# Local scores and AV as full 128x128 matmuls in batches 1 to 3, with loads and casts of batches 2 and 3 at other places

## The chip, the cores and the metric

The kernel runs on one core of a Trainium2 chip. The metric is the device time of one execution in microseconds, of which three runs of the kernel before are given below. A core has five engines with an instruction stream each: TensorE (PE, matmuls, with weight loads shown apart as PEld), VectorE (DVE), ScalarE (ACT), GpSimd (POOL) and SyncE (SP, which issues most of the DMAs here). PE writes to PSUM, eight banks of 512 fp32 columns on 128 partitions; ACT and DVE read it from there.

## What is computed

Block-sparse attention, and a gated feed-forward layer behind it. Shapes: 4 batches, 8 heads, 768 positions, head size 64; d_model 512, d_ff 2048.

```python
k_sum = k.reshape(B, H, nb, 32, D).max(axis=3)          # 24 block maxima of the keys
v_sum = v.reshape(B, H, nb, 32, D).mean(axis=3)         # 24 block means of the values
scores_l = where(|pos_q - pos_k| < 16, scale * q @ k.T, -1e9)
scores_s = scale * q @ k_sum.T + log(32)
a = softmax(concat([scores_l, scores_s]))
attn = a @ concat([v, v_sum])
x = attn, heads side by side                            # 3072 x 512
h = x @ w_in
out = (h * sigmoid(beta * h)) @ w_out
```

## The kernel before

**Attention of one batch.** The 768 positions are cut into 12 query tiles of 64 (`QT`). A tile needs a window of 96 keys (`NK`) and the 24 block maxima, 120 columns, padded to 128: `kw[g][:, m, :]` holds them for tile m of head pair g (`G` = 4 pairs; the two heads of a pair lie on partitions 0 to 63 and 64 to 127). `scores` (L429) makes, for one pair and one half u of the positions (a *score unit*), twelve matmuls of 64 rows by 64 columns into a two-bank PSUM tile `big[..]`, head h in bank h; `weigh` (L443) takes the Exp on ACT into a tile `e`, and `mask_e` (L449) multiplies by the band mask on DVE. `av_mm` (L503) multiplies blocks of e of 64 queries with the values: `ve` holds them in windows for even tiles, `vo` for odd ones (shifted by 64, made by DMAs from `ve`), with a column of ones for the softmax sum and, on partitions 96 to 119, the block means. The means come from `vm_all` (L481, 28 matmuls of 32 columns), are copied to `vm_sb` by DVE and ACT in turn, and spread into `vo` and `ve` by `spread` (L491, DVE). `av_pair` (L863) does both halves of a pair, and `norm` (L529) divides on DVE. `x_dma` (L549) turns the result into `xT` by a transposing DMA (one pair in batch 3 by PE, `x_both`). Batch 0 has forms of its own (`scores0`, `av_split`).

**Feed-forward of one batch.** `h_tile` (L602) makes 16 tiles of h (PE, then Silu on ACT). The product with w_out is a plain one for most of batch 0 (`o_atom`, L623, four matmuls of 512 columns) and else seven half-size products (`product`, L661, eight matmuls of 256 columns each; numbers 1 to 7), for which `h_sums` (L647) and `w_sums` (L655) make sums of quarters on DVE, and `gather` (L682) adds the results up on ACT, DVE and POOL. Products go to PSUM tiles `one0`, `one1`, `acc0`, `acc1`; `SLOTS` says which: 4 goes to acc0, 3 and 5 to acc1. acc0 also serves `vm_all` in batches 2 and 3.

**Order.** A list `main` of steps (8 of `h_two`, 16 of `h_half`, 16 of `o_atom`, 7 products, and for each later batch 16 of `h_step` and 21 products) is run in turn. Everything else is a side step with a place in the table `AT` (L12): a side step at 28.05 is emitted behind main step 28. Each engine runs its instructions in the order emitted and waits for what they need, so a place in the table sets the order on every queue, not a time. So the o_atoms are steps 24 to 39, the h stage of batch 1 is steps 47 to 62, its products 63 to 83, and so on, 37 steps a batch. Names in `AT`, with the batch as the last letter: kl, ql, vl loads (SP); kc, qc, vc casts (POOL); kd, qd transposing DMAs (SP); win, kx, ks build `kw` and the maxima (DVE, DVE, POOL); vo the shifted values; sc, mk, vm, sp, av, xd the steps above; hs, ws the sums.

Of the kernel before, what the change touches and what calls it, by code (L numbers as in the profile page):

```python
# [17 lines left out]
    'clear': [6.428, 6.644],  # L18
    'kt': [10.122, 8.68],
    'km': [17.109, 13.223, 16.831, 23.85],  # L20
    'qt': [26.508, 26.967],
    'late': [32.254],
    'ws': [23.447, 26.164, 38.352, 39.431],
    'hs0': [36.284, 36.98, 42.604, 40.783],
    'vc1': [26.849, 25.757, 27.058, 30.017],
    'vo1': [27.153, 26.475, 30.624, 30.427],
    'exp1': [26.482],
    'sc1': [28.05, 28.06, 30.05, 30.06, 31.438, 31.448, 33.219, 33.904],
    'mk1': [28.082, 28.092, 30.899, 30.909, 32.558, 32.75, 33.826, 34.448],
    'silu1': [34.957],  # L30
    'vm1': [30.622],
    'sp1': [31.039, 33.384],
    'av1': [35.473, 35.88, 37.299, 37.483],
    'xd1': [36.323, 36.794, 40.874, 39.001],
    'hs1': [52.172, 56.695, 58.36, 62.056, 63.409],
    'kl2': [31.49, 27.509, 31.14, 31.359],
    'ql2': [44.528, 45.846, 48.477, 49.061],
    'vl2': [48.656, 50.666, 53.32, 55.633],
    'kc2': [46.766, 47.002, 48.913, 52.382],
    'kd2': [47.896, 48.564, 50.287, 53.981],  # L40
    'win2': [48.822, 54.925, 59.06, 64.294],
    'kx2': [50.116, 57.618, 60.611, 66.447],
    'ks2': [57.494, 58.64, 61.796, 70.807],
    'qc2': [47.142, 55.572, 56.241, 59.845],
    'qd2': [53.645, 55.686, 56.34, 64.339],
    'vc2': [60.103, 63.811, 64.371, 63.63],
    'vo2': [60.676, 64.705, 67.24, 64.464],
    'exp2': [62.362],
    'sc2': [64.902, 64.912, 67.132, 67.349, 69.423, 69.507, 71.144, 71.507],
    'mk2': [64.907, 67.547, 69.019, 69.041, 70.656, 70.74, 74.611, 74.621],  # L50
    'silu2': [83.261],
    'vm2': [69.738],
    'sp2': [70.773, 71.834],
    'av2': [73.1, 73.251, 76.15, 76.759],
    'xd2': [73.535, 75.753, 77.844, 80.713],
    'hs2': [88.697, 93.491, 96.096, 98.876, 99.837],
    'kl3': [70, 68.576, 66.104, 68.383],
    'ql3': [85.72, 83.832, 83.154, 85.128],
    'vl3': [87.046, 86.957, 91.359, 92.448],
    'kc3': [83.124, 84.172, 85.522, 85.86],  # L60
    'kd3': [83.91, 86.33, 85.635, 89.794],
    'win3': [91.341, 93.68, 91.196, 100.991],
    'kx3': [93.659, 96.229, 96.044, 103.349],
    'ks3': [93.765, 97.224, 99.448, 104.103],
    'qc3': [90.383, 91.035, 87.741, 88.767],
# [15 lines left out]
    'mask2': [46.27],  # L81
# [21 lines left out]
def kernel(  # L103
# [39 lines left out]
    NEG = -30000.0  # L143
    assert d_model == H * D and out.shape == (B * S, d_model) and NK + nb <= P
# [104 lines left out]
    mask = const.tile([P, NT, QT], bf16, name="mask")  # L249
# [44 lines left out]
    def more_masks():  # L294
        nc.vector.tensor_copy(out=mask[:], in_=band[:, None, :].to_broadcast([P, NT, QT]))
        nc.vector.memset(mask[0:W, 0], 0.0)
        nc.gpsimd.affine_select(out=mask[:, NT - 1], in_=mask[:, NT - 1], compare_op=ALU.is_ge, fill=0.0,
                                base=QT + W - 1, pattern=[[0, QT]], channel_multiplier=-1)
        nc.vector.memset(mask[NK:NK + nb], 1.0)

    mask2 = const.tile([P, NT, QT], bf16, name="mask2")

    def turn_mask():
        nc.vector.tensor_copy(out=mask2.rearrange("p m (c f) -> p m c f", c=2), in_=mask.rearrange("p m (f c) -> p m c f", c=2))

# [6 lines left out]
    qn = [const.tile([P, S], bf16, name=f"qn{g}") for g in range(G)]  # L312
# [116 lines left out]
    def scores(b, g, u, bg):  # L429
        s = big[bg]  # L430
        for j in range(HT):
            m = u * HT + j
            for h in range(2):
                o = s[:, h, j * QT:(j + 1) * QT]
                if b > 1:
                    nc.tensor.matmul(o.rearrange("p (c f) -> p c f", c=2), kw[g][h * D:(h + 1) * D, m, :], q_tile2(g, h, m),
                                     start=True, stop=True)
                else:
                    nc.tensor.matmul(o, kw[g][h * D:(h + 1) * D, m, :], q_tile(g, h, m), start=True, stop=True)
# [529 lines left out]
```

## Time and profile before

| | |
|---|---|
| three runs | 215.21, 216.53, 216.9 us; median 216.53 us |
| span of the profiled execution | 213.4 us, clock 1.00 |
| its time outside the span | not given; median less span is 3.1 us |
| busy, share of the span | PE 95%, PEld 66%, DVE 65%, ACT 56%, POOL 29% |
| instructions | 5774 |

The page of the profile has the busy time of each engine, the span in 40 slices, the DMA queues, the chain of work that ended last, and the costliest groups. A timeline row has start, length, engine, line, operation, tiles written and read, shapes and count; in brackets the idle time before it and what ended that. A matmul's length in the trace is a latency, some 0.2 us; what a stream of them costs is read from start to start. The chain before goes through PE for 54% of the span, DVE 14%, DMA 14%.

### The profile page before, as it was taken

How to read it: one execution, taken by the hardware profiler on the slowest of the kernel's cores; microseconds unless marked ns; L12 is line 12 of the kernel's file. 1: busy time of each engine (PE TensorE's matmuls, PEld its weight loads, DVE VectorE, ACT ScalarE, POOL GpSimd, SP SyncE). 2: the span in 40 equal slices, each digit the busy share in tenths (PEclk: the TensorE clock that was granted, in tenths of full speed). 3: DMA queues.
4: the chain of work that ended last, by engine and by line, in shares of the span. 5: the costliest groups of instructions: out<-in, count | busy, mean ns of one | idle time of the engine just before them, and what ended most of it. 6: DMA issues, size and time to landing. Idle time of an engine off the chain costs nothing.

```text
span 213.4 us, 5774 instructions
## 1 busy us (share of the span) xinstructions
PE 202.9 (95%) x2393; PEld 140.1 (66%) x2393; DVE 139.5 (65%) x323; ACT 119.0 (56%) x182; POOL 62.0 (29%) x94
## 2 busy tenths in 40 slices
PE   7778999999998999999999999999999999999993
PEld 2366856565554586556888875667788855668882
DVE  4297574799839992677889920999789704464232
ACT  2246986579489121966883137778772229772210
POOL 7609990002620009423520153461600100000111
PEclk9999999999999999999999999999999999999999
DMA  6998999999877995999979999999834820000242
GB/s 119 183 219 150 185 207 207 206 208 214 113 187 199 243 202 179 236 152 202 170 152 223 194 272 272 210 193 194 123 129 27 185 99 3 0 0 3 98 98 98
DMA packets 78393, 33.92 MB, mean 159 GB/s; under 512 B 60688, under 2 KB 75424, under 8 KB 78368
## 3 DMA queue, kind: packets, MB, share of 16 engines
q1 hardware_dynamic: 61968, 23.92, 55.2%
q0 software_dynamic: 7424, 7.34, 21.4%
q10 hardware_dynamic: 8976, 2.30, 7.3%
q8 instruction: 18, 0.29, 0.6%
q14 instruction: 7, 0.06, 0.1%
HBM read 27.37 MB, written 6.29 MB: 158 GB/s over the span
## 4 chain that ended last, share of the span: by engine, by line
PE 54%; DVE 14%; DMA 14%; SPq 5%; ACT 4%; issue 4%; POOL 3%; POOLq 0%; DVEq 0%
PE big L600 18%; PE one L664 11%; PE acc L664 8%; DMA vst<-in_v_dram 8%; PE big L578 4%; PE one L615 3%; DMA krow<-in_k_dram 3%; ACT e L447 3%; DVE kw L371 2%; DVE w_out_sb L337 2%; DMA qst<-in_q_dram 2%; DVE km L357 2%; DVE e L451 2%; POOL ve L456 1%; SPq L210 1%
## 5 line engine op out<-in xcount | busy, mean ns | idle before, releaser
L600 PE MATMUL big<-xT,w_in_sb 128*128 128x384 bf16 x360 | 60.5, 326 | 0.0
L600 PEld LDWEIGHTS <-w_in_sb 128*128 128x128 bf16 x384 | 37.5, 98 | 25.1 <-issue 0.7
L611 ACT ACTIVATE h_sb<-big,beta_sb 128x768 bf16<-128x768 f32 x45 | 39.6, 904 | 25.7 <-PE big L600 25.6
L664 PEld LDWEIGHTS <-h_sb 128*128 128x128 bf16 x320 | 30.6, 98 | 4.9 <-issue 0.5
L645 POOL TENSOR_TENSOR o_sb<-p,u 128x256 f32<-128x256 f32 x10 | 7.3, 727 | 88.9 <-DVE u L645 77.0
L447 ACT ACTIVATE e<-big,bias 128x768 bf16<-128x768 f32 x32 | 27.3, 900 | 6.2 <-PE big L426 4.3
L664 PE MATMUL one<-w_out_sb,h_sb 128*128 128x256 bf16 x240 | 30.4, 273 | 0.2 <-ACT p L368 0.2
L664 PEld LDWEIGHTS <-s_sb 128*128 128x128 bf16 x240 | 23.2, 98 | 2.8
L645 DVE TENSOR_TENSOR s_sb<-h_sb 128x768 bf16<-128x768 bf16 (+2 forms) x16 | 7.8, 487 | 23.5 <-ACT h_sb L611 23.5
L645 DVE TENSOR_TENSOR u<-one,p 128x256 f32<-128x256 f32 x20 | 8.4, 422 | 15.8 <-PE one L664 15.5
L456 POOL CAST ve<-vst 128x832 bf16<-128x832 f32 (+2 forms) x16 | 14.1, 901 | 14.9 <-DMA vst<-in_v_dram 12.5
L368 ACT COPY o_sb<-one 128x256 f32<-128x256 f32 (+1 forms) x14 | 6.1, 433 | 18.4 <-PE one L664 10.0
L451 DVE TENSOR_TENSOR e<-e,mask 128x768 bf16<-128x768 bf16 x24 | 13.7, 597 | 3.9 <-ACT e L447 3.6
L615 PE MATMUL one<-w_out_sb,h_sb 128*128 128x512 bf16 x64 | 15.2, 380 | 0.0
L365 POOL COPY kw<-km 128x288 bf16<-128x288 bf16 x12 | 7.5, 628 | 24.1 <-DVE km L357 14.4
L361 DVE TENSOR_REDUCE km<-kT 128x24 bf16<-128x768 bf16 x12 | 11.2, 944 | 1.8 <-ACT kT L368 1.8
L538 DVE TENSOR_TENSOR xn<-big,r 128x768 bf16<-128x768 f32 x12 | 11.5, 957 | 0.4
L578 PE MATMUL big<-xT,w_in_sb 128*128 128x384 bf16 x64 | 11.7, 327 | 0.0
L664 PE MATMUL acc<-t_sb,h_sb 128*128 128x256 bf16 x80 | 10.9, 273 | 0.0
L568 POOL CAST qn<-qst 128x768 bf16<-128x768 f32 x8 | 7.4, 938 | 10.2 <-DMA qst<-in_q_dram 6.9
L664 PE MATMUL one<-t_sb,s_sb 128*128 128x256 bf16 x80 | 10.4, 273 | 0.0
L664 PE MATMUL acc<-t_sb,s_sb 128*128 128x256 bf16 x80 | 10.4, 273 | 0.0
(145 smaller groups left out, 309.1 us busy)
## 6 DMA issues: line engine op xcount, KB each, us to landing
out_dram<-o_sb SPq DMA_DIRECT2D x19, 256.0 KB, 2.7
vst<-in_v_dram SPq DMA_DIRECT2D x13, 336.0 KB, 5.1
kst<-in_k_dram SPq DMA_DIRECT2D x8, 384.0 KB, 5.0
qst<-in_q_dram SPq DMA_DIRECT2D x8, 384.0 KB, 4.6
w_in_sb<-in_moe_w_in_dram POOLq DMA_DIRECT2D x4, 512.0 KB, 8.0
w_out_sb<-in_moe_w_out_dram POOLq DMA_DIRECT2D x4, 512.0 KB, 13.1
vo<-ve SPq DMA_DIRECT2D x12, 107.2 KB, 2.4
vst<-in_v_dram SPq DMA_DIRECT2D x3, 416.0 KB, 7.1
```

The costliest lines, as they stand in the source:

```text
L361: nc.vector.tensor_reduce(out=km[g][:, NK:NK + nb], in_=kT[g][:, W:W + S].rearrange("p (n f) -> p n f", f=block), op=ALU.max, axis=AX.X)
L365: eng.tensor_copy(out=kw[g][:, :, NK:NK + nb], in_=km[g][:, None, NK:NK + nb].to_broadcast([P, NT, nb]))
L447: nc.scalar.activation(out=e[:], in_=s[:, :, 0:HS], func=ACTF.Exp, bias=bias[:, 0:1], scale=scale)
L451: nc.vector.tensor_mul(out=e.rearrange("p h (m q) -> p h m q", q=QT), in0=e.rearrange("p h (m q) -> p h m q", q=QT), in1=(mask2 if b > 1 e ...
L456: eng.tensor_copy(out=ve[:, g, lo:hi, 0:D], in_=vst[g][:, lo:hi])
L538: nc.vector.tensor_mul(out=x[:, 3 * us[0]:3 * us[0] + 3 * n].rearrange("p (k j) h d -> p k (j h) d", k=n), in0=tv[:, :, :, 0:D], in1=r[:, ...
L578: nc.tensor.matmul(t[:, 0:HS], w_in_sb[:, ki, i * P:(i + 1) * P], xT[:, ki, 0:HS], start=(ki == 0), stop=(ki == k1 - 1))
L600: nc.tensor.matmul(o, w_in_sb[:, ki, i * P:(i + 1) * P], x, start=(ki == 0), stop=(ki == k1 - 1))
L611: nc.scalar.activation(out=o, in_=t, func=ACTF.Silu, scale=beta_sb[:, i:i + 1])
L615: nc.tensor.matmul(t[:, 0:hi - lo], h_sb[:, n, ms * P:(ms + 1) * P], w_out_sb[:, n, lo:hi], start=(n == 0), stop=(n == k2 - 1))
L645: eng.tensor_tensor(out=o, in0=a, in1=b, op=op)
L664: nc.tensor.matmul(SLOTS[n], a[:, j, t * P:(t + 1) * P], b[:, j], start=(j == 0 and n not in (2, 3, 7)), stop=(j == J2 - 1), skip_group_ch ...
```

## The change

Scores of batches 1 to 3 use a query tensor `qz` that holds, for each pair, head 0 on the upper partitions and zeros below, then zeros above and head 1 below. One matmul over all 128 rows then gives both heads: six matmuls of 128 columns a unit instead of twelve of 64. The tiles of a unit go to the two banks in turn by their parity. The Exp is written into blocks of `epad` that have zeros between them, so that a 128-column piece holds the queries of an even tile and zeros, or zeros and those of an odd tile; AV of a pair of tiles is then two full matmuls that add up in PSUM (start, stop) instead of two of 64 columns side by side. There are as many AV matmuls as before. `qz` and `epad` are cleared once (`clear_q`, `clear_e`, and a memset at the start). In batch 1 the q copies from PSUM are four of half the partitions on ACT and four on DVE; in batches 2 and 3 the transposing DMA writes as before, and `q_fix` moves the second head over on DVE and clears its place on POOL. The masks have 14 tiles instead of 12, and move to the pool that is closed at `late_tiles`; the turned mask is made early. Four tiles of e serve batches 1 to 3 (six batch 0) instead of eight, and three output tiles instead of four.

```diff
-    'clear': [6.428, 6.644],
+    'clear': [5.9, 6.644, 6.9, 6.1, 7.2, 7.3],
-    'qt': [26.508, 26.967],
+    'qt': [24.4, 24.5],
-    'ws': [23.447, 26.164, 38.352, 39.431],
+    'ws': [27.0, 27.5, 33.7, 39.431],
-    'sc1': [28.05, 28.06, 30.05, 30.06, 31.438, 31.448, 33.219, 33.904],
+    'sc1': [28.1, 28.6, 29.9, 30.6, 33.1, 33.6, 34.7, 35.3],
-    'av1': [35.473, 35.88, 37.299, 37.483],
+    'av1': [32.9, 34.6, 36.6, 37.9],
...
-    'ql2': [44.528, 45.846, 48.477, 49.061],
+    'ql2': [32.0, 33.0, 34.0, 38.5],
-    'win2': [48.822, 54.925, 59.06, 64.294],
+    'win2': [48.0, 48.9, 49.8, 50.7],
-    'vc2': [60.103, 63.811, 64.371, 63.63],
+    'vc2': [43.5, 44, 44.5, 45.5],
-    'sc2': [64.902, 64.912, 67.132, 67.349, 69.423, 69.507, 71.144, 71.507],
+    'sc2': [64.5, 64.9, 66.1, 66.8, 70.9, 72.2, 74.0, 75.0],
-    'vm2': [69.738],
+    'vm2': [68.2],
-    'av2': [73.1, 73.251, 76.15, 76.759],
+    'av2': [70.4, 73.0, 76.4, 78.0],
-    'vc3': [95.284, 91.652, 97.814, 103.191],
+    'vc3': [79, 80, 81, 82.5],
...
+    def clear_q(gs):
+        nc.vector.memset(qz[D:P, 0, gs], 0.0)
+    def clear_e():
+        for n in range(NE[1]):
+            nc.vector.memset(epad[:, n, :, 1], 0.0)
...
+    epad = eb.rearrange("p (n a b q) -> p n a b q", n=NE[1], b=3, q=QT)
...
+    def q_fix(g):
+        nc.vector.tensor_copy(out=qz[D:P, 1, g], in_=qz[D:P, 0, g])
+        nc.gpsimd.memset(qz[D:P, 0, g], 0.0)
...
-            for h in range(2):
-                o = s[:, h, j * QT:(j + 1) * QT]
...
-                    nc.tensor.matmul(o, kw[g][h * D:(h + 1) * D, m, :], q_tile(g, h, m), start=True, stop=True)
+            o, q = s[:, j % 2, j // 2 * P:(j // 2 + 1) * P], qz[:, :, g]
...
+            nc.tensor.matmul(o, kw[g][:, m, :], q, start=True, stop=True)
...
+    def av_mm(b, g, u, t):
+        tv = t[:, 0:AVW].rearrange("p (j h e) -> p j h e", j=3, h=2)
+        e = et[(b, g, u)][1].rearrange("p a b q -> p a (b q)")
+        for j in range(3):
+            for h in range(2):
+                for par in range(2):
+                    nc.tensor.matmul(tv[:, j, h], e[:, 2 * j + h, par * QT:par * QT + P],
+                                     (vo if par else ve)[:, g, h * J6 + 3 * u + j, 0:D + 1], start=(par == 0), stop=(par == 1))
+        release(b, g, u)
...
+    SB = (2, 1, 2, 1, 2, 1, 1, 2)
...
-    at("qt", [lambda i=i: qt_pe(1, (2 * i, 2 * i + 1), 1 + i, (dve_cp, act_cp)) for i in range(2)])
+    at("qt", [lambda i=i: qt_pe(1, (i, i + 2), 1 - i, (act_cp, dve_cp)[i]) for i in range(2)])
-        at("av" + n, [lambda g=g, b=b: av_pair(b, g, big[1 + g % 2]) for g in range(G)])
+        at("av" + n, [lambda g=g, b=b: av_pair(b, g, big[(1 + g % 2) * (b > 1)]) for g in range(G)])
```

`SB` is the two-bank tile of each score unit. By the last line the AV pairs of batch 1 all write big0, where `vm_all` of batch 1 also goes.

How the rows move, at three places. First DVE ahead of batch 1's scores, from the second copy of x in batch 0 to the scaling of w_out; qz is the query tensor, eb the storage of the Exps, mask_173 the turned mask. Before:

```order
L371 COPY xT<-one_79 128x2x384
L295 COPY mask<-band 128x768
L296 MEMSET mask 16x32
L299 MEMSET mask 24x768
L337 TENSOR_SCALAR w_out_sb<-w_out_sb,inv_beta 128x512 x4
```

Now:

```order
L312 MEMSET eb 128x6x32 x4
L384 COPY xT<-one_76 128x2x384
L296 COPY mask<-band 128x896
L297 MEMSET mask 16x64
L300 MEMSET mask 24x896
L305 COPY mask_173<-mask 128x896
L308 MEMSET qz 64x768 x2
L350 TENSOR_SCALAR w_out_sb<-w_out_sb,inv_beta 128x512 x4
```

The turned mask and two memsets have come in ahead of the scaling, and so of all key work behind it.

Second, DVE in batch 1 from the q copies on; e or eb are the Exps, vm_sb the block means, t_sb the sums of `w_sums`. Before:

```order
L371 COPY qn_177<-big_80 128x768
L371 COPY qn_179<-big_81 128x768
L451 TENSOR_TENSOR e<-e,mask 128x768 x2
L371 CAST vm_sb<-big_85 32x2x64 x2
L451 TENSOR_TENSOR e<-e,mask 128x768 x2
L496 COPY vo<-vm_sb 32x2x6x64 x2
L496 COPY ve<-vm_sb 32x2x6x64 x2
```

Now:

```order
L384 COPY qz<-big_82 64x768 x4
L686 TENSOR_TENSOR t_sb<-w_out_sb 128x2048
L686 TENSOR_TENSOR t_sb<-w_out_sb,t_sb 128x2048
L481 TENSOR_TENSOR eb<-eb,mask 128x2x6x64 x3
L384 CAST vm_sb<-big_82 32x2x64 x2
L481 TENSOR_TENSOR eb<-eb,mask 128x2x6x64
L525 COPY vo<-vm_sb 32x2x6x64 x2
L525 COPY ve<-vm_sb 32x2x6x64 x2
```

The q copies are four, and the two t_sb sums, which stood ahead of them, now stand between them and the masks. Further on in the same stretch, from the masks of pair 3 (s_sb is a sum of `h_sums`, xn the normed result, here of pair 2), now:

```order
L481 TENSOR_TENSOR eb<-eb,mask 128x2x6x64 x2
L686 TENSOR_TENSOR s_sb<-h_sb 128x8x128
L578 RECIPROCAL r<-big_82 128x12
L579 TENSOR_TENSOR xn<-big_82,r 128x768
L686 TENSOR_TENSOR s_sb<-s_sb,h_sb 128x8x128
```

Before, the first of these sums stood behind the norms of pairs 0 and 1, and each norm read a big tile of its own turn; now the norm of pair 2 stands behind the masks of pair 3 and a sum.

Third, DVE in batch 2 around `vm_all`, whose result is in acc_1797 or acc_1789, the tile of product 4; u is the sum that product 7 ends in. Before:

```order
L645 TENSOR_TENSOR u_1931<-one_79,p_1821 128x256
L645 TENSOR_TENSOR o_sb<-acc_1797,u_1931 128x256
L645 TENSOR_TENSOR o_sb<-acc_1798,u_1867 128x256
L451 TENSOR_TENSOR e<-e,mask_176 128x768 x2
L371 CAST vm_sb<-acc_1797 32x2x64 x2
```

Now:

```order
L686 TENSOR_TENSOR u_1898<-one_76,p_1814 128x256
L686 TENSOR_TENSOR o_sb<-acc_1789,u_1898 128x256
L384 CAST vm_sb<-acc_1789 32x2x64 x2
L525 COPY vo<-vm_sb 32x2x6x64 x2
L525 COPY ve<-vm_sb 32x2x6x64 x2
L686 TENSOR_TENSOR o_sb<-acc_1790,u_1841 128x256
```

By 'vm2' at 68.2, PE makes `vm_all` straight behind step 68, which is product 7 of the first third; before, product 3 and two score units stood in between. DVE's read of acc and its copy of the means now follow each other.

166 lines of the change are left out of this document (92 added, 74 removed).

## Prediction

> **What bounds the kernel now.** I read the clock and span first, then the stretches, PE's instructions in order of time, the chain, and last the waits and the groups by form. One core, clock 1.00, span 213.4 us. The three runs have a median of 216.53 us (215.21 to 216.9), so 3.1 us lie around the span; I make the sum on the span and add 3.1. About 1%, 2.2 us, is what a measurement of this kernel can tell from no change.
>
> ```profile
> 40.00:58.00 18.00, 17.49 (x209) 10.55 (x208) 17.84 (x33) 11.97 (x21) 4.24 (x6) 1.00 1.18 189
> 58.00:75.00 17.00, 15.77 (x275) 8.80 (x274) 12.50 (x29) 11.45 (x17) 1.87 (x3) 1.00 0.88 201
> ```
>
> A row gives the stretch, its length, and the busy us of PE, PEld, DVE, ACT and POOL. PE is all but full, so what is added to PE is added to the end. From 40 to 58 us DVE is full too (17.84 of 18.00): two engines bind there at once. Scores and AV of batches 1 to 3 stand in three stretches, whose edges PE's timeline gives:
>
> ```profile
> 52.20 0.59 PE L615 MATMUL one<-w_out_sb,h_sb 128*128 128x512 bf16 x2
> 80.39 0.81 PE L600 MATMUL big<-xT,w_in_sb 128*128 128x384 bf16 x4
> 101.36 0.82 PE L664 MATMUL acc<-t_sb,h_sb 128*128 128x256 bf16 x6
> 125.09 0.81 PE L600 MATMUL big<-xT,w_in_sb 128*128 128x384 bf16 x4
> 146.07 0.60 PE L664 MATMUL acc<-t_sb,h_sb 128*128 128x256 bf16 x4
> 170.46 0.81 PE L600 MATMUL big<-xT,w_in_sb 128*128 128x384 bf16 x4
> ```
>
> A (batch 1, beside the output product of batch 0) is 28.19 us, B (batch 2 beside the products of batch 1) 23.73, C 24.39. What a burst of small matmuls costs there:
>
> ```profile
> 103.00 0.27 PE L664 MATMUL one<-w_out_sb,h_sb 128*128 128x256 bf16 x1
> 103.20 0.52 PE L436 MATMUL big<-qn,kw 64*128 64x64 bf16 x24
> 103.66 1.05 PE L664 MATMUL one<-t_sb,s_sb 128*128 128x256 bf16 x8
> ...
> 68.60 0.88 PE big L511 x48
> ```
>
> Two score units (24 matmuls on half the rows) take 0.46 us from start to start, 19 ns each: two run side by side. Products follow each other every 0.109 us (8 in 0.87), but 0.20 pass before the burst: 0.10 to empty the array as the tile shape changes; leaving it is inside the 0.46. An AV burst of 48 takes 0.88 the same way. A batch has four score bursts and two AV bursts: 4 x 0.56 + 2 x 0.98 = **4.2 us** of PE.
>
> **The change: PE's work.** Scores become 48 matmuls of 128 columns on all rows, AV 96 with a 128x128 stationary block and 65 columns, neither of them tiled. Both shapes stand in the trace elsewhere:
>
> ```profile
> 35.97 0.50 PE L860 MATMUL one<-identity,xn 128*128 128x128 bf16 x6
> L860 PE MATMUL one<-identity,xn 128*128 128x128 bf16 x12 | 1.0, 219 | 0.0
> 23.54 0.35 PE L519 MATMUL one<-vm_one,e 128*128 128x65 bf16 x6
> L519 PE MATMUL one<-vm_one,e 128*128 128x65 bf16 x24 | 1.4, 194 | 0.0
> ```
>
> Six in 0.50 of which the last is 0.219: 56 ns a step. Six in 0.35, the last 0.194: 31 ns. So scores 48 x 56 = 2.7, AV 96 x 31 = 3.0, and the block means of v (vm_all, 32 columns wide, still tiled) now pay their own 0.1: **5.8 us, +1.6 a batch, +4.9 in all**. The emptying that goes (six times 0.1 in, and as much out) is already in this: full matmuls do twice the array work that two tiles shared. Bounds: the step can't fall under the column rate (0.109 / 256 = 0.43 ns: 54 and 28 ns; -0.4 a batch), and AV's pairs, which now add into one bank, could cost the 56 ns of the other shape (+2.4 a batch). I take 31, the same shape on the same e.
>
> [...]
>
> **Waits that go.** The two long ones, and what else stands in A:
>
> ```profile
> 54.88 1.55 PE L384 MATMUL big<-identity,qrow 96*64 96x96 bf16 x64
> ...
> 58.89 0.53 PE L439 MATMUL big<-qn,kw 64*128 64x64 bf16 x24 [0.62 <-ACT qn L368]
> 59.35 1.90 PE L615 MATMUL one<-w_out_sb,h_sb 128*128 128x512 bf16 x8
> 61.18 0.52 PE L439 MATMUL big<-qn,kw 64*128 64x64 bf16 x24
> 61.63 0.58 PE L485 MATMUL big<-ve,A_avg 128*32 128x128 bf16 x28
> ...
> 66.42 0.35 PE L439 MATMUL big<-qn,kw 64*128 64x64 bf16 x12 [0.44 <-ACT e L447]
> ```
>
> 59.35 to 61.18 is 1.83 for eight output matmuls and the change of shape: 0.217 each, 0.87 for four. In A 64 of them, 56 products at 0.109, the q transposes (1.6 with their change of shape), vm_all (0.5) and the 4.2 make 26.3 of 28.19: 1.9 are waits. In B 168 products (18.4), vm_all and the 4.2 leave 0.7, in C, with 0.3 for x_both, 1.0. I let all 3.6 us go: q is now copied by ACT before its Exp table, keys and values of batches 2 and 3 come some 20 steps earlier, and kw and km are built in the h stages, not between the masks. If nothing new waited, the span would grow by 4.9 - 3.6 = 1.3.
>
> **Waits that come, A.** DVE is the engine queued up there, and the change adds to it ahead of its scale and key work:
>
> ```profile
> L299 DVE MEMSET mask<- 24x768 bf16 x1 | 0.7, 698 | 0.4 <-POOL mask L297 0.4
> L304 DVE COPY mask<-mask 128x768 bf16<-128x768 bf16 x1 | 0.6, 550 | 0.0
> 56.20 1.81 DVE L371 COPY qn<-big 128x768 bf16<-128x768 bf16 x2
> ```
>
> clear_q is two memsets of 768 words (0.70 each, time going by words, not partitions), the turned mask 0.55 x 14/12 = 0.64, longer masks 0.1: +2.1. The q copies are now four of half the partitions and the same 768 columns: 0.87 a piece, +1.7. Two more stand in waits that DVE has anyway:
>
> ```profile
> DVE xT L371 <- PE one L860: 1.6, 2, 0.9
> DVE beta_sb L325 <- PE one L324: 1.4, 1, 1.4
> ```
>
> clear_e (four of 192 words, 0.7) fits the wait for x_two (half of 1.6), the memset of qz at the start (1536 words, 1.4) that for beta; uncovered they cost at most their length once. DVE was through with q and the first two T sums at 58.0; the order is changed, the sum not, so now 61.85. Then come:
>
> ```profile
> 63.58 0.29 DVE L371 CAST vm_sb<-big 32x128 bf16<-32x128 f32 x1 [1.03 <-ACT vm_sb L368]
> 63.90 1.03 DVE L451 TENSOR_TENSOR e<-e,mask 128x768 bf16<-128x768 bf16 x2
> 64.94 0.63 DVE L496 COPY vo<-vm_sb 32x768 bf16<-32x768 bf16 x2
> 65.49 0.62 DVE L496 COPY ve<-vm_sb 32x768 bf16<-32x768 bf16 x2
> ```
>
> three masks (1.5), the vm_sb pair with ACT's copy between (0.9), a mask (0.5), spread(0) (1.2): 66.0. PE reaches AV of pair 0 at 52.2 + 9 x 0.87 + 1.6 + 4 x 0.34 + 0.6 + 0.2 = 63.8. **It waits 2.2.** Behind it on PE stand the scores of pairs 2 and 3, so ACT runs dry too. Next late is AV of pair 3: all four AV pairs now use the one tile big0, and the norm of pair 2 stands on DVE behind both masks of pair 3 and an h sum. From 66.0 PE needs 8.0 to get there (74.0). ACT meanwhile:
>
> ```profile
> 64.67 3.28 ACT L447 ACTIVATE e<-big,bias 128x768 bf16<-128x768 f32 x4
> 70.70 3.00 ACTq L553 DMA_TRANSPOSE xT<-xn  x2
> ```
>
> two Exps of pair 2 until 69.9, x_dma of pair 0 on ACT's own queue 1.3 to 1.5 (71.2), an Exp (72.0), an o_sb copy (72.6), an Exp (73.5); DVE then masks (74.0), h sum 0.7, norm 1.2: 75.85. **PE waits 1.8** more, and 0.2 at the third score unit. A: +1.6 - 1.9 + 4.2 = **+4.0**.
>
> **Waits that come, B and C.** vm_all writes acc0 and now stands straight behind product 7, whose sum DVE still has to read from acc0:
>
> ```profile
> 108.00 0.42 DVE L645 TENSOR_TENSOR u<-one,p 128x256 f32<-128x256 f32 x1 [0.23 <-PE one L664]
> 108.45 0.77 DVE L645 TENSOR_TENSOR o_sb<-acc,u 128x256 f32<-128x256 f32 x2
> ```
>
> The product's last result, u 0.42, o_sb 0.42 and two hand-overs are 1.2, with nothing else on PE: **1.2**. Before, product 3 and two score units stood between. Two products (1.75) later AV of pair 0 needs spread(0): vm_sb 0.3 on DVE, 0.3 on ACT, 0.3 on DVE, four copies 1.2, hand-over 0.2 make 2.3: **0.6**. B: products 18.4, scores and AV 5.7, vm_all 0.6, waits 1.8 = 26.5, **+2.7**; C the same and x_both 0.3: 26.8, **+2.4**.
>
> Other edits at nothing: loads and transposes on SP end some 10 us ahead of their readers (were they late, PE would wait for a landing); q_fix (four copies, four POOL memsets a batch) lies under the 21 us h stage. Below nothing none can pay: PE's edges of the h stages hold no wait. x transposes could land later among more loads; 8 us of products and h parts cover them.
>
> The mask product on blocks of 64 is the one open price. Low: unchanged. High: one element a cycle, as norm's 0.96 against 0.48. I take unchanged, by the nearer row, two-byte sums in chunks of 128, 0.68 for 1024:
>
> ```profile
> L538 DVE TENSOR_TENSOR xn<-big,r 128x768 bf16<-128x768 f32 x12 | 11.5, 957 | 0.4
> L645 DVE TENSOR_TENSOR s_sb<-h_sb 128x1024 bf16<-128x1024 bf16 x1 | 0.7, 681 | 0.0
> ```
>
> **Sum.** 213.4 + 4.0 + 2.7 + 2.4 = 222.5 span, **225.6 us**.
>
> **Rivals.** (1) The covers hold: DVE reaches spread(0) by 63.8 and hands acc0 over in time. For: DVE has 4.5 us free in 58 to 75. Against: that gap lies behind the added 3.8. 213.4 + 1.3 + 3.1 = 217.8, no change that can be told: the other side, and it decides as soon as each DVE result is out before PE asks.
> (2) The mask product loses its double rate: +0.4 on six masks in A, four each in B and C: +5.6, 231.
> (3) Weight loads don't hide under short matmuls: half-way to the 109 ns of 256 columns, 82 for scores: +3.8, 229.4. [...]
> (4) Tiling costs more than my 0.2 a burst:
>
> ```profile
> PEld L439 <- issue: 2.9, 6, 0.6
> PEld L511 <- issue: 1.6, 6, 0.3
> PEld L436 <- issue: 1.5, 7, 0.2
> ```
>
> 6.0 us of weight-load idleness stand before tiled matmuls, and nothing is named as its cause. If all of it goes (3.4 are in my sum), rates are the bare ones (1.2) and (1) holds: 217.8 - 2.6 - 1.2 = 214.0, faster. Against: PE itself was not idle then.
>
> **How the numbers follow.** Forecast 0.60 (its own range 222 to 228.5: each wait 0.7 either way), (1) 0.17, (2) 0.10, (3) 0.06, (4) 0.07. The range goes down to 217 for (1) and up to 230 for (3) and the near half of (2). Faster is most of (4): 0.06; within 1% (1) and the rest of (4): 0.16; slower 0.78.
>
> **What would show it.** Right: scores 56 ns and AV 31 ns a step, no 0.2 before them; PE waiting near 64 and 74 us for DVE, and after product 7 at vm_all for o_sb in B and C; A, B, C of 32, 26.5, 26.8. Wrong: AV steps over 40 ns, mask products of 0.9, no DVE wait ahead of AV of pair 0, or h stages other than 21 us.

## The result, and the profile after

| | before | after |
|---|---|---|
| runs of both kernels on one chip, median | 216.29 us (215.21 to 216.9) | 252.26 us (250.09 to 253.86) |
| ratio after to before | | 1.162, 95% interval 1.154 to 1.169 |
| span of the profiled execution, granted clock | 213.4 us, 1.00 | 248.4 us, 0.959 |
| stage A / B / C by PE's timeline | 28.2 / 23.7 / 24.4 us | 34.7 / 46.2 / 26.7 us |
| h stage of batch 1 / of batch 2 | 21.0 / 21.0 us | 21.0 / 25.4 us |

Slower, as forecast, but by 36 us and not by 9; the time lies far above the range. The head, the h stage of batch 3 and what follows it are as before (head 51.5 against 52.2 us, end 43.0 in both). All that is lost stands between 51 and 205 us. Ratios, and below the medians of late23 and kdfirst, are of the executions within 1.5% of the fastest of the same kernel. The stretches of the five stages, in the same columns as before (busy us of PE, PEld, DVE, ACT, POOL, then the granted clock, the DMA share and GB/s):

```profile
51.46:86.18 34.72, 29.29 (x352) 19.77 (x356) 29.27 (x52) 17.35 (x26) 9.89 (x12) 0.95 1.00 193
86.18:107.16 20.98, 20.96 (x131) 12.52 (x129) 12.12 (x18) 13.12 (x16) 12.05 (x15) 1.00 0.78 168
107.16:153.34 46.18, 31.63 (x342) 25.64 (x341) 24.16 (x54) 13.72 (x23) 12.45 (x15) 0.85 0.90 175
153.34:178.74 25.40, 22.80 (x131) 13.05 (x129) 15.20 (x30) 13.49 (x17) 7.08 (x10) 0.93 0.33 73
178.74:205.41 26.67, 25.45 (x348) 22.83 (x347) 17.88 (x42) 14.24 (x24) 1.50 (x3) 1.00 0.27 64
```

B (third row) holds 14.6 us in which PE does nothing, and its clock is 0.85; C, with the same products, scores and AV, holds 1.2 at full clock. What PE waited for (the rows of the head left out; a row gives who waited for whom, the us in total, how many times, and the longest), and then the clock in 40 slices:

```profile
PE big L455 <- ACT eb L474: 6.9, 1, 6.9
PE big L550 <- DVE ve L525: 3.6, 2, 2.9
PE one L705 <- DVE s_sb L686: 3.0, 3, 1.3
PE big L550 <- DVE eb L481: 2.9, 2, 2.3
PE one L641 <- ACT o_sb L381: 2.6, 1, 2.6
PE acc L514 <- DVE o_sb L686: 2.1, 2, 1.1
PE big L550 <- DVE xn L579: 1.8, 1, 1.8
```
```profile
PEclk9999999999799999997997688799999999999999
```

The rows ve, o_sb at L514 and xn are the waits of the forecast. The other four, 15.4 us, were not in it; in the kernel before, no wait of PE in these stages was longer than 0.62 us. And the dearest one, step by step, on PE, ACT and POOL in turn:

```profile
128.20 1.04 PE L705 MATMUL one<-w_out_sb,h_sb 128*128 128x256 bf16 x8
136.13 0.82 PE L455 MATMUL big<-qz,kw 128*128 128x128 bf16 x6 [6.90 <-ACT eb L474]
136.75 1.91 PE L705 MATMUL one<-w_out_sb,h_sb 128*128 128x256 bf16 x8
```
```profile
124.55 0.90 ACT L474 ACTIVATE eb<-big,bias 128x768 bf16<-128x768 f32 x1 [1.71 <-PE big L455]
134.90 0.37 ACT L381 COPY p<-acc 128x256 f32<-128x256 f32 x1 [9.45 <-POOL o_sb L686]
135.17 0.91 ACT L474 ACTIVATE eb<-big,bias 128x768 bf16<-128x768 f32 x1
```
```profile
127.56 0.82 POOL L609 CAST qn<-qst 128x768 bf16<-128x768 f32 x1 [4.75 <-DMA kT<-kn]
130.43 0.82 POOL L609 CAST qn<-qst 128x768 bf16<-128x768 f32 x1 [2.04 <-DMA kT<-kn]
133.36 0.82 POOL L609 CAST qn<-qst 128x768 bf16<-128x768 f32 x1 [2.12 <-DMA kT<-kn]
134.15 0.72 POOL L686 TENSOR_TENSOR o_sb<-p,u 128x256 f32<-128x256 f32 x1
```

Read from below. POOL has an output sum of batch 1 to make (134.15), but three casts of batch 3's q stand ahead of it. Each waits until a transposing DMA of k has ended, because the five buffers of cast keys and queries are taken and only that DMA frees one. ACT's copy p waits 9.45 us for POOL's sum (it writes the tile that the sum reads), the Exp of a score unit stands behind the copy, and PE waits 6.90 us for the bank which that Exp reads. The links between are work of batches 1 and 2 that runs there, but what holds them up is a cast whose reader runs two stages later.

The last PE row shows a second loss: eight products take 213 ns each (1.70 from 136.75 to 138.45) where the eight at 128.20 take 109. PE's clock has halved; the row of the stretch gives a granted clock of 0.50 (the number behind PE's busy time):

```profile
134.08:140.90 6.82, 4.77 (x30) 0.50 0.36 68
```

### The profile page after: what moved, and what is told of

Same layout as the page of the kernel before. It is cut to its first block, busy times and chain, and to the rows that moved or that the text cites. A ratio compares the mean times of both kernels' runs of the same rounds, so it can differ in the third digit from the quotient of the medians.

```text
span 248.4 us, 5521 instructions
## 1 busy us (share of the span) xinstructions
PE 215.6 (87%) x2244; PEld 152.1 (61%) x2249; DVE 150.5 (61%) x340; ACT 121.6 (49%) x184; POOL 68.9 (28%) x102
## 4 chain that ended last, share of the span: by engine, by line
PE 56%; DVE 22%; DMA 10%; issue 4%; ACT 3%; SPq 2%; POOL 1%; ACTq 1%; POOLq 0%; DVEq 0%
PE big L641 23%; PE one L705 10%; PE acc L705 9%; PE big L619 3%; DVE eb L481 3%; PE big L550 2%; DMA vst<-in_v_dram 2%; DVE kw L384 2%; DMA krow<-in_k_dram 2%; DVE s_sb L686 2%; DVE w_out_sb L350 2%; PE one L641 2%; DMA kT<-kn 2%; DVE qz L384 2%; ACT eb L474 1%
## 5 line engine op out<-in xcount | busy, mean ns | idle before, releaser
L641 PE MATMUL big<-xT,w_in_sb 128*128 128x384 bf16 x360 | 61.8, 330 | 0.0
L652 ACT ACTIVATE h_sb<-big,beta_sb 128x768 bf16<-128x768 f32 x45 | 39.6, 905 | 26.9 <-PE big L641 26.8
L474 ACT ACTIVATE eb<-big,bias 128x768 bf16<-128x768 f32 x32 | 28.0, 902 | 18.1 <-PE big L455 8.9
L705 PEld LDWEIGHTS <-h_sb 128*128 128x128 bf16 x320 | 32.0, 102 | 4.9
L705 PE MATMUL one<-w_out_sb,h_sb 128*128 128x256 bf16 x240 | 31.4, 280 | 0.0
L705 PEld LDWEIGHTS <-s_sb 128*128 128x128 bf16 x240 | 23.8, 102 | 7.1 <-DVE s_sb L686 3.7
L686 DVE TENSOR_TENSOR s_sb<-h_sb 128x768 bf16<-128x768 bf16 (+2 forms) x16 | 8.4, 525 | 24.5 <-ACT h_sb L652 24.4
L481 DVE TENSOR_TENSOR eb<-eb,mask 128x768 bf16<-128x768 bf16 x24 | 14.9, 639 | 10.7 <-ACT eb L474 10.6
L550 PE MATMUL big<-ve,eb 128*128 128x65 bf16 x144 | 11.5, 197 | 8.4 <-DVE ve L525 3.6
L455 PE MATMUL big<-qz,kw 128*128 128x128 bf16 x144 | 12.3, 234 | 7.4 <-ACT eb L474 6.9
L550 PEld LDWEIGHTS <-eb 128*128 128x128 bf16 x288 | 11.1, 100 | 11.0 <-DVE ve L525 3.4
L455 PEld LDWEIGHTS <-kw 128*128 128x128 bf16 x144 | 10.5, 106 | 9.9 <-ACT eb L474 7.2
L609 POOL CAST qn<-qst 128x768 bf16<-128x768 f32 x8 | 7.5, 932 | 26.9 <-DMA kT<-kn 25.7
L609 POOL CAST kn<-kst 128x768 bf16<-128x768 f32 x8 | 7.6, 960 | 22.1 <-DMA kst<-in_k_dram 15.1
L381 ACT COPY p<-acc 128x256 f32<-128x256 f32 x10 | 3.7, 371 | 20.5 <-PE acc L705 11.0
```

Of the source, the lines that this page charges most:

```text
L455: nc.tensor.matmul(o, kw[g][:, m, :], q, start=True, stop=True)
L474: nc.scalar.activation(out=o, in_=i, func=ACTF.Exp, bias=bias[:, 0:1], scale=scale)
L481: nc.vector.tensor_mul(out=e, in0=e, in1=(mask2 if b > 1 else mask)[:, 2 * u:2 * u + NT].rearrange("p (b a) q -> p b a q", b=2))
L550: nc.tensor.matmul(tv[:, j, h], e[:, 2 * j + h, par * QT:par * QT + P], (vo if par else ve)[:, g, h * J6 + 3 * u + j, 0:D + 1], start=(par ...
L609: eng.tensor_copy(out=t[:], in_=stg[(nm, b, g)].rearrange("p h j d -> p j h d"))
L641: nc.tensor.matmul(o, w_in_sb[:, ki, i * P:(i + 1) * P], x, start=(ki == 0), stop=(ki == k1 - 1))
```

## The experiments

Each kernel ran in rounds with the kernel before on the same chip; ratios are against that. Stages are those of the profiled execution; h1 and h2 are the h stages of batches 1 and 2, ahead of B and of C. Theory 1 says that the new places cost the time, theory 2 that the new forms do.

| kernel | median us | ratio (95%) | A | B | h2 | C |
|---|---|---|---|---|---|---|
| after | 252.26 | 1.162 (1.154 to 1.169) | 34.7 | 46.2 | 25.4 | 26.7 |
| places | 239.84 | 1.106 (1.097 to 1.115) | 29.5 | 43.9 | 22.9 | 24.4 |
| late3 | 241.91 | 1.111 (1.100 to 1.121) | 35.4 | 30.9 | 21.0 | 37.3 |
| late23 | 249.76 | 1.152 (1.140 to 1.163) | 32.3 | 42.2 | 21.0 | 35.6 |
| late23b | 235.73 | 1.093 (1.082 to 1.103) | 32.3 | 31.4 | 21.0 | 33.1 |
| late23fix | 234.09 | 1.084 (1.074 to 1.093) | 32.9 | 29.9 | 21.0 | 31.6 |
| noqfix | 226.55 | 1.053 (1.046 to 1.061) | 32.3 | 27.0 | 21.0 | 26.9 |
| qcast3 | 253.23 | 1.167 (1.159 to 1.175) | 35.1 | 47.9 | 25.7 | 27.0 |
| kdfirst | 246.80 | 1.141 (1.130 to 1.151) | 32.9 | 45.1 | 25.3 | 26.7 |
| xpe2 | 245.43 | 1.135 (1.126 to 1.145) | 32.9 | 46.9 | 21.0 | 26.7 |
| resched | 236.10 | 1.097 (1.088 to 1.106) | 35.3 | 33.2 | 21.0 | 28.2 |
| reschedvm | 236.51 | 1.098 (1.090 to 1.107) | 32.9 | 34.7 | 21.0 | 28.1 |
| qfixmid | 233.76 | 1.083 (1.075 to 1.090) | 34.0 | 29.3 | 21.0 | 31.0 |
| qfixvm | 230.92 | 1.070 (1.063 to 1.078) | 32.3 | 28.3 | 21.0 | 29.9 |

### Places without forms, forms without places

**places** is the kernel before with only the table's places of the changed kernel:

```diff
-    'ql2': [44.528, 45.846, 48.477, 49.061],
+    'ql2': [32.0, 33.0, 34.0, 38.5],
...
-    'qc3': [90.383, 91.035, 87.741, 88.767],
+    'qc3': [62.0, 65, 66, 67],
```

(and so for kl, vl, kc, kd, win, kx, ks, qd, vc, vo of batches 2 and 3).

> The kernel before, with its own matmul forms and masks, and only the steps of batches 2 and 3 (loads, casts, transposes, key steps) at the places of the changed kernel. Theory 1: the same queues are held, 15 to 24 us more than before: 231 to 240 us; less than the changed kernel by the waits of A, and because four output tiles and eight tiles for Exps are left. Theory 2: within 3 us of 216.3.

239.84: theory 1 holds and theory 2 falls. The places alone, with the old matmuls, old masks, eight Exp tiles and four output tiles, cost 22.9 us, and B is 43.9. The chain has the same links. What ACT, POOL and PE waited for in it:

```profile
ACT p L368 <- POOL o_sb L645: 12.1, 1, 12.1
```
```profile
POOL qn L568 <- DMA kT<-kn: 8.8, 3, 4.5
```
```profile
137.35 1.87 PE L664 MATMUL acc<-w_out_sb,s_sb 128*128 128x256 bf16 x8 [8.58 <-ACT p L368]
```

**late3** is the changed kernel with batch 3's steps back at the old places, and q_fix behind its transposes:

```diff
-    'qc3': [62.0, 65, 66, 67],
+    'qc3': [90.383, 91.035, 87.741, 88.767],
...
-    'qf3': [88, 89.2, 90.4, 91.6],
+    'qf3': [93.1, 94.0, 95.0, 96.5],
```

> As the run before, but only batch 3's steps are back at the old places; batch 2's stay early. Theory 1: the 6.9 us wait of PE at 129 and what follows it in B up to 153 go (some 12 us), the wait for s_sb at 110 to 114 (3 to 4 us) stays: B 31 to 35 us, the time 237 to 242. Theory 2: above 248.

241.91, and B is 30.9, as theory 1 had it: the 6.9 us and what came behind are gone from B. That the time lies in theory 1's 237 to 242 too is partly luck: h2, back at 21.0, gave 4.4 us that were not forecast, and C, which was right at 26.7, is now 37.3; the next run shows what holds it. **late23** does the same for both batches:

```diff
-    'qf2': [51.2, 52.4, 53.4, 54.4],
+    'qf2': [54.5, 56.5, 58.5, 64.6],
```

> The changed kernel with every load, cast, transposing DMA and key step of batches 2 and 3 back at the places of the kernel before; q_fix stands behind the transposes of q. The matmul forms and the order of batch 1 stay changed. Theory 1 (the new places cost the time, by holding the in-order queues of SP and POOL): B falls from 46.2 us to 26 to 29, h2 from 25.4 to about 21, A keeps most of its 34.7; sum 252.3 - 17 to 20 - 4 = 228 to 231 us. Theory 2 (the new matmul and Exp forms cost it, by slower steps or a lower clock): B stays above 40 and the time above 245.

249.76, 2.5 less than the changed kernel: theory 1's 228 to 231 is missed by 19 us, and B, at 42.2, and the time both lie where theory 2 had them. What PE waited for, and DVE's timeline, give another reason than the forms:

```profile
PE one L705 <- DVE s_sb L686: 13.6, 6, 3.6
PE big L455 <- POOL kw L378: 4.2, 2, 3.9
```
```profile
104.27 0.36 DVE L417 COPY qz<-qz 64x768 bf16<-64x768 bf16 x1 [9.39 <-DMA qz<-qn]
...
109.45 0.36 DVE L417 COPY qz<-qz 64x768 bf16<-64x768 bf16 x1 [4.33 <-DMA qz<-qn]
```

L417 is q_fix. At the old places the transposed q lands at the end of the h stage, in time for its old reader, PE. q_fix is a new reader on DVE, which runs in order: the copy waits 9.39 and 4.33 us, and key copies and h sums, for which products wait, stand behind it. So the test of the places was no clean one: it had put q_fix where it holds the sums. **noqfix** and **late23b** separate this. The first leaves q_fix out:

```diff
     def q_fix(g):
+        return
```

> As late23 (matmul forms changed, batches 2 and 3 at the old places) with q_fix left out: the second head's queries of batches 2 and 3 are not moved over and their old place is not cleared, so that part of the computation is missing. If q_fix is what cannot stand at the old places (a reader of the transposed q on DVE's and POOL's in-order queues, ahead of the sums or ahead of the scores), then B and C come out at the forecast's 26.5 and 26.8, up to 1.5 above it, with no wait for s_sb or qz: 222 to 228 us. If the forms themselves cost what late23b still has over the forecast (10 us): 232 to 237.

226.55, against a forecast of 225.6 for the whole change; A, B, C of 32.3, 27.0, 26.9 against 32.2, 26.5, 26.8. By the rounds it is 11.4 us above the kernel before, where the forecast said 9.1. (That execution's head was 54.6 us, with the clock at 0.50 from 17.1 to 23.9, where the same head took 51.4 to 54 in the others, so the stages are the better comparison.) PE's waits of 0.5 us and more in A to C (lines are one higher here, L456 the scores, L515 vm_all, L551 AV):

```profile
PE acc L515 <- DVE o_sb L687: 3.1, 2, 1.8
PE big L551 <- DVE ve L526: 2.3, 1, 2.3
PE big L551 <- DVE xn L580: 1.1, 1, 1.1
PE big L456 <- ACT eb L475: 0.5, 1, 0.5
```

These are the forecast's waits and no others. So the forms and batch 1's order are worth about what the sum said, and the rest, 25.7 us by the medians and 23.4 by the ratios, is q_fix and the places. The places alone cost 22.9 in the old kernel; with these 11.4 that makes 34.3 of the 36.0. If the two add up, q_fix at its new places cost some 2 us; no run left it out there. **late23b** keeps q_fix, behind the h sums:

```diff
-    'qf2': [54.5, 56.5, 58.5, 64.6],
+    'qf2': [63.6, 63.8, 66.9, 69.05],
-    'qf3': [93.1, 94.0, 95.0, 96.5],
+    'qf3': [100.0, 100.2, 103.95, 106.05],
```

> As late23, with q_fix of each pair moved behind the h sums of its stage (it stands ahead of that pair's scores). In late23 its copy on DVE waited 9.4 and 4.3 us for a transposed q, with the key work and the h sums queued behind it, so that run did not test the places alone. Theory 1 (the new places cost the time): B 26 to 28.5 us, C 26 to 28.5, h2 21.0, A 32 to 35: 225 to 231 us. Theory 2 (the forms): above 242.

235.73, 5 above the upper end of theory 1 and 6 below theory 2's 242: neither. The waits for s_sb are gone, and a wait for q_fix's other half is there, its clear on POOL:

```profile
109.22 0.83 PE L455 MATMUL big<-qz,kw 128*128 128x128 bf16 x12 [2.03 <-POOL qz L418]
109.89 1.84 PE L705 MATMUL one<-t_sb,s_sb 128*128 128x256 bf16 x8
```

2.03 us here (3.7 in C), and after each some 16 products at half clock, 1.5 us: the eight of the second row take 1.64. Ahead of the sums q_fix holds DVE, behind them PE.

### Is there a free place for q_fix?

**qfixmid** moves it in between the last sums, where q has just landed, and one cast of v behind it:

```diff
-    'qf2': [63.6, 63.8, 66.9, 69.05],
+    'qf2': [62.0, 63.6, 66.9, 69.05],
-    'qf3': [100.0, 100.2, 103.95, 106.05],
+    'qf3': [97.7, 99.5, 100.3, 104.5],
```

> As late23b (all steps of batches 2 and 3 at the old places, q_fix kept), with q_fix of the first pairs moved forward to where their transposed q has landed, in between the last h sums and not behind them, and in batch 3 one cast of v (and the DMA of its shifted values) moved behind them on POOL; nothing is left out. If the 9 us between late23b (235.7) and noqfix (226.6) are PE's waits for q_fix's clear on POOL (2.2 us in B, 3.7 in C) and the half clock that follows them (1.5 each): 226 to 230 us. If q_fix costs as much wherever it stands, by DVE's and POOL's time: 233 to 237.

233.76, 2 less than late23b: the second reading's 233 to 237, by which q_fix costs as much wherever it stands, and not the 226 to 230 of a price that is only waits for the clear. No wait for qz is left, but the wait at vm_all has grown from 2.1 us to 6.9. **qfixvm** moves vm_all, the spread, AV of pair 0 and the first scores of pair 2 back (and so in batch 3):

```diff
-    'vm2': [68.2],
+    'vm2': [69.2],
-    'av2': [70.4, 73.0, 76.4, 78.0],
+    'av2': [71.4, 73.0, 76.4, 78.0],
```

> As qfixmid, with vm_all of batches 2 and 3 behind product 3 and the spread, AV of pair 0 and the first scores of pair 2 moved with it. In qfixmid PE's waits for q_fix are gone, but PE now waits 2.8 us in B and 4.1 in C at vm_all for a sum of DVE, which is full there with q_fix, key copies and masks. If that wait is the rest of q_fix's price and can be covered by product 3 and a score unit: 2 to 5 us less, 228.5 to 232. If DVE's time itself is the bound there: within 1.5 us of qfixmid's 233.8.

230.92, 2.8 less. What PE waited for at vm_all, in qfixmid and then in qfixvm:

```profile
PE acc L514 <- DVE o_sb L686: 6.9, 2, 4.1
```
```profile
PE acc L514 <- DVE o_sb L686: 5.1, 2, 3.2
```

The move covered 1.8 of the 6.9 us; the wait for a full DVE stays. Part of the 2.8 is not the move's: A, where nothing changed, went from 34.0 to 32.3 because a stretch of half clock there (67.2 to 70.6) is missing in qfixvm. So q_fix still stands some 4 us above noqfix, and 7 with vm_all at noqfix's early place (qfixmid). **late23fix** tried the same move on late23b, and in batch 1 the T sums behind the first masks:

```diff
-    'ws': [27.0, 27.5, 33.7, 39.431],
+    'ws': [32.4, 33.7, 35.6, 39.431],
```

> As late23b, with three more things moved: in batch 1 the T sums on DVE behind the first masks and the spread; in batches 2 and 3 vm_all behind product 3 instead of product 7, and with it the spread, AV of pair 0 and the first scores of pair 2. If the waits at these places are what the forecast says (3.0 and 1.95 in A, 1.2 and 0.6 in B and in C) they shrink and 4 to 7 us go: 219 to 226. If DVE's and PE's work there is the bound and waits only change their place: within 2 us of late23b.

234.09, 1.6 less, and not the 4 to 7: it is the other reading, by which waits only change their place. B and C each gave 1.5 (31.4 to 29.9, 33.1 to 31.6), but only in C by shorter waits (5.7 to 4.3 us). In B the waits are no shorter (4.3 and 4.6); what is gone there is late23b's stretch of half clock (109.95 to 113.37). A gave nothing (32.9 for 32.3): the wait for the spread shrank, one of 2.2 us for a later norm came.

### Which part of the held queues?

Three one-part repairs of the changed kernel. **qcast3** takes POOL's casts of q from ahead of its sums:

```diff
-    'qc3': [62.0, 65, 66, 67],
+    'qc3': [78, 79, 79.5, 80],
```

> The changed kernel with one line other: the casts of batch 3's q on POOL stand at 78 to 80 instead of 62 to 67, behind the output sums of B that POOL makes. Theory 1 in its narrow form (a cast that waits for a buffer holds POOL, POOL's sum o_sb comes late, ACT's copy p behind it and the Exp behind that, and PE waits 6.9 us): the 6.9 us go, with some of the 2.3 and 0.6 behind them and of the half clock: 8 to 14 us, 238 to 244. Theory 3 (the DMA engines are simply full in B, so that any order ends as late): less than 3 us gained, 249 to 253.

253.23: nothing gained, so the narrow theory is not enough. By its time alone it fits theory 3, that the DMA engines are full in B. Against that, in the changed kernel they moved 157 GB/s in the stretch of the 6.9 us wait (128 to 136 us), where they had moved 238 just before (118 to 128); no run took traffic away at the new places, so a part of theory 3 stays open. The 6.9 us wait for ACT is gone, in its place stand a wait of 12.9 and behind it, on DVE and POOL, another link:

```profile
PE big L550 <- DVE eb L481: 13.2, 2, 12.9
```
```profile
DVE o_sb L686 <- DMA out_dram<-o_sb: 14.8, 1, 14.8
```
```profile
POOL o_sb L686 <- DMA out_dram<-o_sb: 23.6, 1, 23.6
```

The output sums want a free output tile, of which three are left; the store that frees one stands on SP behind batch 3's transposes and loads of v. **kdfirst** puts the loads of v behind the transposes of k:

```diff
-    'vl3': [62.5, 63.5, 64.5, 65.5],
+    'vl3': [65.3, 65.4, 65.5, 65.6],
```

(and vl2 to 42.9 to 43.2).

> The changed kernel with the loads of v of batches 2 and 3 behind the four transposes of k on SP, instead of among or ahead of them. Theory 1a and 1b: the casts of q get their buffers at once and the transposes of k are issued before those of x: 5 to 13 us go, 239 to 247. Theory 3 (DMA engines full, the order on SP matters little): 249 to 254.

246.80, 5.5 less by the medians and 3.0 between the profiled executions, at or below the low end of the 5 to 13 expected. Of the 3.0, 1.8 is A, which has lost its stretch of half clock behind an equal wait (2.85 us); B gave 1.1. The casts wait less, but the stores now stand behind eight loads of v, and POOL waits for one of them:

```profile
POOL o_sb L686 <- DMA out_dram<-o_sb: 11.5, 1, 11.5
```

**xpe2** makes the x transposes of batch 2 on PE:

```diff
-    'xq2': [-0.681, -0.396, -0.684, -0.009],
+    'xq2': [-1.5, -1.5, -1.5, -1.5],
```

The reason for it was this wait of SP's queue in the changed kernel (105 to 160 us):

```profile
SPq L613 <- DMA xT<-xn: 11.0, 3, 5.7
```

> The changed kernel with the x transposes of batch 2 made by PE (24 more transposes of 128 columns, four copies on DVE) instead of transposing DMAs on ACT's queue; the loads stay at the new places. Theory 1a (the transposing DMAs on SP and on ACT wait for each other's end, which the profile shows as 11.0 us of SP waiting for xT, and they hold SP's stores and loads and ACT's Exps): B loses 8 to 14 us: 238 to 245. Theory 1b (the circle is only casts that wait for buffers which SP's transposes behind loads of v free): within 3 us of 252.3, or above it by PE's and DVE's work (up to 4).

245.43, 6.8 less, but not by the expected way: SP waits for xT no more and h2 is back at 21.0 (25.4 in the changed kernel), while B is 46.9. A, at 32.9, lost its half clock as in kdfirst, with its wait of 2.87 us as it was: that is no gain of this edit. The chain through POOL has stayed in it:

```profile
PE big L601 <- ACT eb L474: 9.5, 1, 9.5
```
```profile
POOL qn L609 <- DMA kT<-kn: 9.1, 3, 4.9
```

So no single link is the cause. Casts holding POOL, stores held on SP and transposes waiting for each other stand side by side, and in each of the three repairs another one of them set the end of B. **resched** takes all three out of A and B, with kd, most of qc, qd, vl, win, kx, ks, qf, vc and vo of batches 2 and 3 in the h stage, while k and q are still loaded early:

```diff
-    'kd3': [62.2, 63.2, 64.2, 65.2],
+    'kd3': [83.05, 83.06, 83.07, 83.08],
-    'qc3': [62.0, 65, 66, 67],
+    'qc3': [62.0, 84.0, 84.2, 84.4],
-    'qf3': [88, 89.2, 90.4, 91.6],
+    'qf3': [92.0, 93.0, 94.2, 95.4],
```

> The changed kernel with q_fix, and the transposes of k and q, most casts of q and the loads of v of batches 2 and 3 at places in the h stage, behind the x transposes and the stores of the stage before and ahead of the h sums; the loads and casts of k and the loads of q stay early. Theory 1 (what stands among the x transposes and output sums of A and B costs the time, by POOL held by casts, SP held by transposes, output tiles held by late stores): B 26.5 to 29, C 26.5 to 29, h2 21: 223 to 230 us. If a new hold comes in the h stage (q_fix or key copies late, as in late23): 235 to 250.

236.10, at the low end of the second band (235 to 250), and by its way. C is 28.2, inside theory 1's 26.5 to 29. B is 33.2: in h1 q_fix again waits for its q (3.79 us, the longest) and holds the sums (PE waits 5.6 us for s_sb, 4.5 of it in B). **reschedvm** adds qfixvm's move of vm_all:

```diff
-    'vm2': [68.2],
+    'vm2': [69.2],
```

> As resched, with vm_all of batches 2 and 3 behind product 3 and the spread, AV of pair 0 and the first scores of pair 2 moved with it. In late23fix this made B and C 1.5 us shorter each (31.4 to 29.9 and 33.1 to 31.6). If that wait is of its own: 2 to 3.5 us less than resched, so 220 to 227. If it hid behind others there: within 1 us of resched.

236.51, no gain, as for a wait that hides behind others: in B the wait for s_sb, ahead of vm_all's, is 1.5 longer and swallows it; in C, at 28.1, what is won at vm_all (1.2 to 0.3 us) returns as a wait for a norm (0.6) and for s_sb.

No version beat the kernel before; the nearest that computes everything is qfixvm, 7% slower.

## Why the prediction was wrong

**The step that failed** is the paragraph behind "Waits that come, B and C": "Other edits at nothing: loads and transposes on SP end some 10 us ahead of their readers", and "q_fix ... lies under the 21 us h stage". I priced some 90 moved steps by their distance in the table to their readers. What counts on an in-order queue is what stands behind them while they wait. Batch 2's casts of q waited so already ahead of h1:

```profile
POOL qn L609 <- DMA kT<-kn: 25.7, 5, 16.3
```

16.3 us in one wait, with k's transposes going out at 91 to 96 us on SP, behind loads of v. So keys, q_fix and then h sums were late on DVE, and B began with 3.0 us of waits for s_sb. The front's sentence that a place sets an order and not a time was the warning; the forecast used places as times. And q_fix had a cost that the forecast could have read: at the old places the transposed q lands within a few us of its scores, so "under the h stage" held only if the loads came earlier, which they could not without these collisions. The measured price of both together is 252.3 - 226.6 = 25.7 us, most of it the places'.

**The half clock** was not in the sum: it is a term put at nothing. In the five stages PE is idle 21.9 us more than before (23.8 for 1.9) and busy 13.7 us more (130.1 for 116.4). Of the 13.7, the new work is 4.5, as noqfix shows (120.9; forecast 4.9). PE also worked 17.6 us at a granted clock of 0.50, in stretches from 65.8 to 161.4 us; half of that, 8.8 us, is an estimate of what the half clock cost. noqfix, with waits of at most 2.3 us in these stages, has no such stretch there.

When the clock halves can be read from the clocks of the runs. In each run the times at which the granted clock changes lie a multiple of 3.41 us apart (here 65.81, 69.22, 113.60, 117.01, 134.08, 140.90, 147.73, 151.14, 157.97, 161.38). In windows on that grid, PE's idle time within one window all but tells the two apart: in the changed kernel and the 13 others of the table, from 45 us to 8 us before the end, all 30 windows at full clock that half clock followed have 1.94 us or more of idle time, and the 674 others 1.98 at most. (In the changed kernel alone the five that half clock followed, from 62.40, 110.19, 130.67, 144.32 and 154.55 us on, have 2.07 to 3.41, the others at full clock 1.55 at most. In the heads, with many smaller matmuls, less was enough: 1.26 us in qfixvm.) So the same wait of 2.03 us, for q_fix's clear, was followed by half clock in late23b, where it lies in one window, and not in late23fix, where two share it:

```profile
106.54:109.95 3.41, 1.38 (x20) 1.00 0.84 164
```
```profile
106.19:109.60 3.41, 2.72 (x22) 1.00 1.35 211
109.60:113.02 3.42, 2.09 (x26) 1.00 0.51 101
```

PE is busy 1.38 of 3.41 us in the first, 2.72 and 2.09 in the others. Whether a wait of 2 to 3 us cost a stretch of half clock thus hung on where the grid fell; in A it came and went between kernels whose A is the same (34.0 us with it in qfixmid, 32.3 without in qfixvm). This is read from the traces; no run here filled a wait with other work to prove it.

**What was right.** Scores and AV at full clock:

```profile
108.90 0.83 PE L455 MATMUL big<-qz,kw 128*128 128x128 bf16 x12
109.57 0.60 PE L705 MATMUL one<-t_sb,s_sb 128*128 128x256 bf16 x4
...
127.48 0.19 PE L550 MATMUL big<-ve,eb 128*128 128x65 bf16 x1
...
128.17 0.19 PE L550 MATMUL big<-vo,eb 128*128 128x65 bf16 x1
```

12 scores in 0.67 are 56 ns a step (forecast 56), 24 AV in 0.72 are 30 (forecast 31), and no 0.2 stands before them. In the kernel before, a burst of scores or AV starts 0.20 us after the start of the 256-column product ahead of it (103.00 to 103.20; 0.202 to 0.205 at all eleven such places), where products follow each other at 0.109; here, at full clock, it is 0.11 (108.79 to 108.90). That the array empties in this time was the forecast's reading; the traces show the time alone. C, beside which no later batch is loaded, came out at 26.7 for 26.8. noqfix's idle time of PE in the five stages is 7.4 us, where the forecast's waits (4.2, 1.8 and 1.8) make 7.8. The 3.1 us that the sum adds around the span was too much: 250.09 us stand over a span of 248.4, which is 1.7. In A both named waits are there, ahead of AV of pairs 0 and 3:

```profile
66.42 0.24 PE L550 MATMUL big<-ve,eb 128*128 128x65 bf16 x1 [2.86 <-DVE ve L525]
77.60 0.19 PE L550 MATMUL big<-ve,eb 128*128 128x65 bf16 x1 [1.78 <-DVE xn L579]
```

2.86 for 2.2 and 1.78 for 1.8; in noqfix, 2.3 and 1.1. A's 34.7 for 32.2 is mostly the first wait's 0.7 and 1.1 of half clock (66.8 to 69.1); kernels whose A has the same steps of batch 1 stood at 32.3 to 35.4, with the half clock in the upper ones only (late3 35.4, resched 35.3; not in xpe2 and kdfirst, 32.9). The forecast's 1.2 at vm_all in B and C came out at 1.0 each.

**The rivals.** None came. The covers did not hold (1); the mask products took 0.55 us undisturbed, as before, and not norm's 0.96 (2; these are times, no trace counts cycles); the steps were the rows' (3); untiling saved no more than was summed, as C shows (4). No rival had the moved transfers as its mechanism, although the forecast named in a subordinate clause what would happen "were they late": that clause should have been the rival of slower, with POOL's o_sb and SP's stores named as what stands behind.

## What to carry to other kernels

A step moved earlier on an in-order queue is priced by its own wait and by who stands behind it, not by how early it is for its reader: for each, ask which buffer, store or transfer it waits for, and what of the running stage is queued next on that engine. A new reader of an old transfer (here a copy on DVE ahead of PE) is late wherever the old reader was just in time. When several held queues run side by side, repairing one can show little or nothing; test the places against the forms first, as a whole, and only then look for the links. Compare runs by stage, and by wait and clock in each, before an edit is credited: some 1.7 us of half clock came and went with the phase of a window.

## What the runs showed of the hardware

**A mask product beside POOL.** The same product of 768 two-byte elements takes 0.55 us alone; beside POOL's casts of v it took up to 1.22 (least, median and most ns of the 24, then two of them on DVE, then POOL's casts). Five of the 24 took 0.63 to 1.22, and each ran beside an instruction of POOL; but five more ran beside a cast of k and took 0.55 to 0.56. In each of the slow five POOL's instruction had begun first (as the first cast here, at 145.25, ahead of the product that starts at 145.65), in each of the others the product had:

```profile
L481 DVE TENSOR_TENSOR eb<-eb,mask x24: 546/558/1224, 61.9 to 198.2; 128x768 bf16<-128x768 bf16 x24
```
```profile
144.86 2.01 DVE L481 TENSOR_TENSOR eb<-eb,mask 128x768 bf16<-128x768 bf16 x2
```
```profile
145.25 3.19 POOL L485 CAST ve<-vst 128x832 bf16<-128x832 f32 x3
```

**Transposing DMAs of two queues followed each other.** In the changed kernel SP's transposes of k and q waited 11.0 us for ACT's of x to end; the kernel before, where SP's stood in the h stages, had no such row. With the x transposes on PE (xpe2) the row is gone. So a transposing DMA that is moved into a stage with others can be a wait on its queue, not only traffic. No run here shows whether the two could run side by side.
